# Linear attention and a gated feed-forward block on one core: both halves of the second batch turned by DMA, its work and the loads around it moved to other slots

## Chip, cores and metric

One Trainium2 chip, one core. The metric is the device time of one execution of the whole program, in microseconds (us). Each kernel is executed several times and the median is given. The profile is of one execution.

## What is computed

There are two stages. The first is attention with the keys and values projected along the sequence from 1024 to 64 rows. Its result, 8192 tokens of 512 values, is the input of a gated feed-forward block.

```python
k_proj = np.einsum('ks,bhsd->bhkd', E, k)           # q, k, v: 8 x 8 x 1024 x 64, f32
v_proj = np.einsum('ks,bhsd->bhkd', F, v)
scores = scale * np.matmul(q, k_proj.transpose(0, 1, 3, 2))
scores = scores - np.max(scores, axis=-1, keepdims=True)
attn = np.exp(scores)
attn = attn / (np.sum(attn, axis=-1, keepdims=True) + 1e-09)
attn_out = np.matmul(attn, v_proj)
x = attn_out.transpose(0, 2, 1, 3).reshape(8192, 512)
g = x @ w_gate                                      # 512 x 1536
silu = g * (1.0 / (1.0 + np.exp(-g)))
out = (silu * (x @ w_val)) @ w_out                  # 1536 x 512, f32 out
```

## The kernel before

**The loop that everything hangs on.** The feed-forward part is cut into 16 chunks of 512 tokens, two for each of the 8 batches, and each chunk into 12 column blocks of 128. So there are 192 steps `t`; chunk `c` is `t // 12`. Chunks 0 and 1 are batch 0, chunks 2 and 3 batch 1, and so on. A step does four matmuls of 512 columns for the gate (`f_g`, L324, tile gps), then four for the value (`f_v`, L324, tile vps), and then zero to two portions of four matmuls for the output of the chunk before (`f_y`, L362, tile yps). ScalarE takes a tanh of gps (L336), VectorE makes the hidden tile hT from it (L343, L348). When three portions are done, ScalarE copies the block to ysb (L372), and SyncE (SP) writes it to DRAM (L374).

**Slots.** Attention for the coming batches is spread over the steps by hand. Slot `2t` is run between `f_g` and `f_v` of step `t`, slot `2t+1` after its output portions. `put(s, fn, ...)` lays a unit into slot `s`. The program runs under a manual schedule, so each engine's queue is in the order in which the program is written down; only semaphores order engines against one another. Within a slot, loads come first and the rest in the order of the calls of `put`. Units, each for a batch b and a half ch or an eighth j (four eighths to a half):

- `load_k`, `load_v`, `load_q`: loads with a cast from f32 to bf16, issued by GpSimd (POOL) at L88, L98 and L107. k and v have 1 MB each after the cast, a half of q 0.5 MB. All go through the queue that the profile calls q0, software_dynamic. The weights (L117, L123) go through it as well, ahead of the steps. Buffers: two for k, two for v, four for halves of q.
- `u_KV`: projects k, v or both (L149). ScalarE copies the k part to `ks`, VectorE the v part to BDV.
- `u_KT`: four small transposes of `ks` on TensorE (L174), and four VectorE copies to BD.
- `u_T`: four transposes of 128x128 of q on TensorE into the tile qTp (L195), and a copy to the tile qT by ScalarE.
- `u_TD`: the same turn of a whole half of q by one DMA issued from SP (L207), to the tile qTd.
- `u_S`: four score matmuls with 128 columns (L229) with qT or qTd as weights, and an exponential on ScalarE (L233, tile ee).
- `u_R`: row sums and reciprocals on VectorE (L244, L246). `u_N`: the normalisation on POOL (L260), to the tile AA for one eighth, or AAd for a whole half.
- `u_A`: four transposes of AA on TensorE into the tile aTp (L276), and a copy to AT by VectorE.
- `u_AD`: the same turn of a whole half by one DMA issued from SP (L214), from AAd to AT.
- `u_PV`: one matmul of 512 columns (L287) with BDV as weights, and a copy to xT, the input of the feed-forward part, by ScalarE.

SP's queue thus holds turns and output blocks in program order, and POOL's queue holds normalisations and load issues in program order. An instruction that waits holds up all that stand behind it in its own queue. The DMA turns go through the same queue as the output blocks, the profile's q1, hardware_dynamic.

**Which halves are turned how.** `BY_DMA` lists the halves that go through `u_TD` and `u_AD`. Its trailing `[1:]` leaves out (1, 0): the first half of the second batch goes through `u_T` and `u_A` on TensorE, as all of batch 0 does; the other 13 halves are turned by DMA. `place(b)` puts a batch's units into slots. Chunk 2, the first to need batch 1, begins at slot 48.

Of the kernel before, what the change touches and what calls it, by code (L numbers as in the profile page):

```python
# [15 lines left out]
B = 8  # L16
# [11 lines left out]
CH = 2  # L28
CW = 512
NIT = B * CH * NFT  # L30
BY_DMA = [(b, ch) for b in range(1, B) for ch in range(CH)][1:]


@with_exitstack
def kernel(
# [49 lines left out]
    def load_k(b, h0=0, h1=H):  # L85
        if b:
            kb[b] = kv_pool.tile([P, H, NJ, D], BF16, name="kb", tag="kb")
        nc.gpsimd.dma_start(  # L88
            out=kb[b][:, h0:h1].rearrange("p h j d -> p h (j d)"),
            in_=k[b, h0:h1].rearrange("h (p j) d -> p h (j d)", j=NJ),  # L90
        )
# [11 lines left out]
    def load_q(b, ch, js=(0, 4)):  # L103
        if js[0] == 0:
            qb[b, ch] = q_pool.tile([P, H, 4, D], BF16, name="qb", tag="qb")
        js = slice(*js)
        nc.gpsimd.dma_start(  # L107
            out=qb[b, ch][:, :, js, :].rearrange("p h j d -> p h (j d)"),
            in_=q[b].rearrange("h (p c j) d -> p c h j d", c=2, j=4)[:, ch, :, js, :].rearrange(
                "p h j d -> p h (j d)"  # L110
            ),
        )

    def load_w_gv(c0, c1, which=(0, 1)):
        cs = slice(c0 * P, c1 * P)
        for wsrc, wdst in [((moe_w_gate, wg), (moe_w_val, wv))[i] for i in which]:
            nc.gpsimd.dma_start(  # L117
                out=wdst[:, :, cs],
                in_=wsrc[:, cs].rearrange("(t p) c -> p t c", p=P),
            )  # L120

    def load_wo(i):
        nc.gpsimd.dma_start(  # L123
            out=wo[:, 6 * i : 6 * (i + 1), :],
            in_=moe_w_out[6 * i * P : 6 * (i + 1) * P, :].rearrange("(t p) c -> p t c", p=P),
        )
# [5 lines left out]
    def bank(where, shape, dt, name):  # L132
        pool, tag = banks[where]
        return pool.tile(shape, dt, name=name, tag=tag)
# [85 lines left out]
    def u_S(b, u, at="a"):  # L220
        ch, w = divmod(u, 4)
        g, i = divmod(w, 2)
        ps = bank(at, [P, 4, P], FP32, "sc")
        if (b, ch) in BY_DMA:
            t = qT[b, ch, "d"][:].rearrange("p (h i) t -> p i h t", i=2)[:, i, 4 * g : 4 * g + 4]
# [23 lines left out]
    def u_N(b, u):  # L249
        ch, w = divmod(u, 4)  # L250
        g, i = divmod(w, 2)
        if (b, ch) in BY_DMA:
            if (b, ch, "d") not in AA:
# [62 lines left out]
    def f_mm(c, f, w, i=None):  # L316

        if i != 1:
            half[c, f, w] = bank("gv"[w], [P, CW], FP32, "gv"[w] + "ps")
        ps = half[c, f, w]  # L320
        x = xT[divmod(c, CH)]
        ts = slice(0, CW) if i is None else slice(256 * i, 256 * (i + 1))
        for kt in range(NKT):
            nc.tensor.matmul(  # L324
                out=ps[:, ts],
                lhsT=(wg, wv)[w][:, kt, f * P : (f + 1) * P],
                rhs=x[:, kt, ts],
                start=(kt == 0),
                stop=(kt == NKT - 1),
            )  # L330
        return ps
# [57 lines left out]
    def put(s, fn, *a):  # L389
        slots[s].append((fn, a))  # L390

    def place(b):
        s0 = 48 * (b - 1)
        if b == 1:
            put(30, u_TD, 1, 1)
            put(34, u_KV, 1, "k")
            put(36, u_KT, 1)
            put(40, u_KV, 1, "v")
            sa = (37, 38, 39, 40, 48, 50, 52, 54)
            tt = (35, 36, 37, 38)  # L400
            ta = (41, 42, 43, 44)
            put(57, u_AD, 1, 1)
            sp = (43, 44, 45, 46, 66, 67, 68, 69)
        else:
            put(s0, u_KV, b)
            put(s0 + 3, u_KT, b)
            o = 14 if b == 2 else 6
            put(s0 + (3 if b == 2 else -6), u_TD, b, 0)
            put(s0 + (5 if b == 2 else -4), u_TD, b, 1)
            sa = [s0 + o + 3 * j for j in range(NJ)]  # L410
            put(sa[3] + 4, u_AD, b, 0)
            put(sa[7] + 4, u_AD, b, 1)
            sp = [s0 + i for i in (39, 41, 43, 45, 57, 59, 61, 63)]
        for j in range(NJ):
            if (b, j // 4) not in BY_DMA:
                put(tt[j], u_T, b, j)
                put(ta[j], u_A, b, j)
            put(sa[j], u_S, b, j)
            put(sa[j] + 1, u_R, b, j)
            put(sa[j] + 1, u_N, b, j)  # L420
        for i in range(8):
            put(sp[i], u_PV, b, i // 4, i % 4)
# [5 lines left out]
    with tc.manual_schedule():  # L428
# [99 lines left out]
        load_q(0, 1)  # L528
        for f in (6, 8, 10):
            load_w_gv(f, f + 2)  # L530
        load_wo(0)
        load_wo(1)
        load_k(1)
        f_mm(0, 0, 0, 0)
        u_PV2(0, 0, 1, 1, act)
        f_mm(0, 0, 1, 0)
# [10 lines left out]
        put(22, u_PV, 0, 1, 1)  # L547
        put(23, u_PV, 0, 1, 2)
        put(23, u_PV, 0, 1, 3)
        put(20, load_q, 1, 0)  # L550
        put(20, load_v, 1)
        put(20, load_q, 1, 1)
        for b in range(1, B):
            place(b)
        for b in range(2, B):
            s0 = 48 * (b - 1) - (12 if b == 2 else 24)
            put(s0, load_k, b)
            put(s0 + 2, load_v, b)
            put(s0 + 4, load_q, b, 0)
            put(s0 + 6, load_q, b, 1)  # L560

        for s in slots:
            slots[s].sort(key=lambda x: x[0] not in (load_k, load_v, load_q))
# [50 lines left out]
```

The softmax here doesn't subtract the row's maximum and nothing guards it: scores larger than these inputs give would overflow.

## Time and profile before

| what | value |
|---|---|
| median of 4 runs | 572.75 us (572.51 to 573.37) |
| the profiled execution, its own time | 572.75 us |
| its span, first to last instruction | 571.0 us |
| granted TensorE clock in it | 1.0 |
| DVE, ACT, POOL busy | 336.4, 238.3, 109.1 us |
| read from and written to DRAM | 60.29 and 16.78 MB |
| transposes of L195, of L276 | 48 matmuls each |
| DMA turns of L207, of L214 | 13 each |

How to read it. PE is TensorE's matmul side, PEld its loading of weights, DVE VectorE, ACT ScalarE. A timeline row gives the start, the time until the last of its instructions ended, the engine, line, operation, tiles written and read, and how many instructions are in it. Matmuls are pipelined: a row's own length overlaps the row after it, so what a group costs is the distance between its start and the next row's start. For a DMA, the row of the issuing engine tells when it was issued; landing is when its semaphore says that the data is there.

### The profile page before, as it was taken

What the parts mean: (1) busy time and instruction counts of PE and PEld (TensorE: products, weight loads), DVE (VectorE), ACT (ScalarE), POOL (GpSimd) and SP (SyncE); (2) the same over time, 40 slices, a digit from 0 to 9 for tenths busy, and PEclk for the clock granted to TensorE, in tenths of its full rate; (3) what the DMA queues carried; (4) which work ended last, traced back from release to release, by engine and by line L of the source; (5) the groups of instructions that cost most, each with busy time, mean ns of one, the idle gap of its engine ahead of it and who ended that gap; (6) DMA issues with size and microseconds to landing.
All of it is one profiled execution on the core that took longest, in us unless ns stands there. A gap on an engine that the chain in (4) does not pass through costs nothing.

```text
span 571.0 us, 7944 instructions
## 1 busy us (share of the span) xinstructions
PE 564.1 (99%) x2971; PEld 268.5 (47%) x2971; DVE 336.4 (59%) x581; ACT 238.3 (42%) x421; POOL 109.1 (19%) x122
## 2 busy tenths in 40 slices
PE   8999999999999999999999999999999999999997
PEld 4654444444444444444444444444444444444444
DVE  4777466666466654666556664567546675554540
ACT  3565534344435434443335434354343543443232
POOL 6834122134002500124001330023200220000000
PEclk9999999999999999999999999999999999999999
DMA  9999994349902697038940499204990124100012
GB/s 208 178 200 206 201 170 83 87 80 197 201 18 54 106 190 150 19 74 137 195 94 37 69 175 197 59 20 93 189 184 32 46 48 75 38 37 25 32 38 92
DMA packets 106983, 61.86 MB, mean 108 GB/s; under 512 B 60096, under 2 KB 98240, under 8 KB 106944
## 3 DMA queue, kind: packets, MB, share of 16 engines
q0 software_dynamic: 42800, 29.36, 35.8%
q1 hardware_dynamic: 63232, 30.42, 24.8%
q10 hardware_dynamic: 912, 1.57, 0.9%
q8 instruction: 23, 0.38, 0.3%
q14 instruction: 16, 0.13, 0.1%
HBM read 60.29 MB, written 16.78 MB: 135 GB/s over the span
## 4 chain that ended last, share of the span: by engine, by line
PE 92%; DMA 3%; DVE 2%; POOL 1%; ACT 1%; issue 0%; DVEq 0%; POOLq 0%
PE yps L362 29%; PE vps L324 28%; PE gps L324 27%; PE kvp L149 3%; PE sc L229 2%; PE pv L287 2%; DMA wv<-in_moe_w_val_dram 2%; DMA qb<-in_q_dram 1%; DVE zz L244 1%; POOL AA L260 0%; POOL wg L117 0%; PE qTp L195 0%; DVE hT L348 0%; ACT xT L137 0%; DVE s L343 0%
## 5 line engine op out<-in xcount | busy, mean ns | idle before, releaser
L343 DVE SCALAR_TENSOR_TENSOR s<-th,gps 128x512 f32<-128x512 f32 x192 | 130.5, 680 | 139.0 <-ACT th L336 138.6
L324 PE MATMUL gps<-xT,wg 128*128 128x512 bf16 (+1 forms) x776 | 197.8, 377 | 0.4 <-DMA wg<-in_moe_w_gate_dram 0.2
L324 PE MATMUL vps<-xT,wv 128*128 128x512 bf16 (+1 forms) x776 | 197.5, 377 | 0.1
L362 PE MATMUL yps<-wo,hT 128*128 128x512 bf16 (+1 forms) x780 | 194.5, 376 | 0.0
L336 ACT ACTIVATE th<-gps 128x512 f32<-128x512 f32 x192 | 114.6, 597 | 163.1 <-PE gps L324 161.6
L348 DVE TENSOR_TENSOR hT<-s,vps 128x512 bf16<-128x512 f32 x192 | 131.9, 687 | 22.1 <-PE vps L324 1.5
L362 PEld LDWEIGHTS <-hT 128*128 128x128 bf16 x780 | 76.2, 98 | 89.9
L260 POOL TENSOR_TENSOR AAd<-ee,rr 128x512 bf16<-128x512 f32 x52 | 54.1, 1040 | 319.5 <-issue 178.1
L324 PEld LDWEIGHTS <-wv 128*128 128x128 bf16 x776 | 73.8, 98 | 83.2 <-issue 3.3
L324 PEld LDWEIGHTS <-wg 128*128 128x128 bf16 x776 | 74.0, 98 | 81.6 <-DMA wg<-in_moe_w_gate_dram 0.7
L372 ACT ACTIVATE ysb<-yps 128x512 f32<-128x512 f32 (+1 forms) x65 | 38.4, 591 | 78.1 <-PE yps L362 78.1
L137 ACT CAST xT<-pv 128x512 bf16<-128x512 f32 x63 | 36.7, 585 | 51.2 <-PE pv L287 50.3
L244 DVE TENSOR_REDUCE zz<-ee 128x8 f32<-128x512 f32 x64 | 43.4, 679 | 19.4 <-ACT ee L233 19.4
L233 ACT ACTIVATE ee<-sc 128x512 f32<-128x512 f32 x64 | 37.9, 595 | 17.9 <-PE sc L229 17.8
L287 PE MATMUL pv<-AT,BDV 128*128 128x512 bf16 x60 | 22.6, 379 | 0.0
L229 PEld LDWEIGHTS <-qTd 128*128 128x128 bf16 x208 | 16.0, 98 | 12.3
L229 PE MATMUL sc<-BD,qTd 128*128 128x128 bf16 x208 | 20.1, 219 | 0.0
L137 DVE CAST BDV<-kvp 64x256 bf16<-64x256 f32 x14 | 6.0, 427 | 22.1 <-ACT ks L159 19.1
L260 POOL TENSOR_TENSOR AA<-ee,rr 128x512 bf16<-128x512 f32 x11 | 11.4, 1039 | 36.3 <-ACT th L336 18.7
L246 DVE RECIPROCAL rr<-zz 128x8 f32<-128x8 f32 x64 | 13.0, 203 | 6.7 <-DVE zz L244 0.5
L149 PE MATMUL kvp<-vb,FT 128*64 128x512 bf16 (+2 forms) x80 | 15.7, 339 | 0.3 <-ACT BDV L137 0.3
L149 PE MATMUL kvp<-kb,ET 128*64 128x512 bf16 (+1 forms) x72 | 15.5, 358 | 0.2 <-DMA kb<-in_k_dram 0.2
(51 smaller groups left out, 146.1 us busy)
## 6 DMA issues: line engine op xcount, KB each, us to landing
out_dram<-ysb SPq DMA_DIRECT2D x63, 256.0 KB, 2.3
qb<-in_q_dram POOLq DMA_DIRECT2D x15, 512.0 KB, 17.0
kb<-in_k_dram POOLq DMA_DIRECT2D x7, 1024.0 KB, 11.7
vb<-in_v_dram POOLq DMA_DIRECT2D x7, 1024.0 KB, 14.3
wo<-in_moe_w_out_dram POOLq DMA_DIRECT2D x2, 768.0 KB, 15.5
wg<-in_moe_w_gate_dram POOLq DMA_DIRECT2D x5, 256.0 KB, 9.3
wv<-in_moe_w_val_dram POOLq DMA_DIRECT2D x5, 256.0 KB, 9.9
kraw<-in_k_dram ACTq DMA_DIRECT2D x2, 512.0 KB, 4.8
```

What stands on the lines that cost most here:

```text
L137: (nc.scalar.copy if eng is nc.scalar else eng.tensor_copy)(out=out, in_=in_)
L149: nc.tensor.matmul(out=t[lo : lo + 64, h0:h1].rearrange("p h d -> p (h d)"), lhsT=w[:, j, :], rhs=src[b][:, h0:h1, j, :], start=(j == 0), ...
L229: nc.tensor.matmul(out=ps[:, n, :], lhsT=t[:, n, :], rhs=BD[b % 2][:, 4 * g + n, :], start=True, stop=True)
L233: nc.scalar.activation(out=e[:].rearrange("p h j k -> p (h j k)"), in_=ps[:].rearrange("p a k -> p (a k)"), func=AF.Exp, scale=scale,)
L244: nc.vector.reduce_sum(out=z[:], in_=e[:], axis=AX.X)
L260: eng.tensor_tensor(out=a.rearrange("p j h k -> p h j k"), in0=ee.pop((b, u))[:], in1=rr.pop((b, u))[:].unsqueeze(3).to_broadcast([P, 4, 2 ...
L324: nc.tensor.matmul(out=ps[:, ts], lhsT=(wg, wv)[w][:, kt, f * P : (f + 1) * P], rhs=x[:, kt, ts], start=(kt == 0), stop=(kt == NKT - 1),)
L336: nc.scalar.activation(out=th[:], in_=ps[:], func=AF.Tanh, scale=0.5)
L343: nc.vector.scalar_tensor_tensor(out=s1[:], in0=th[:], scalar=1.0, in1=g[:], op0=ALU.add, op1=ALU.mult)
L348: nc.vector.tensor_tensor(out=hT[c][:, f, :], in0=s1[:], in1=ps[:], op=ALU.mult)
L362: nc.tensor.matmul(out=yy[c][:, cs], lhsT=hT[c][:, f, i * P : (i + 1) * P], rhs=wo[:, f, cs], start=(f == 0), stop=(f == NFT - 1),)
L372: nc.scalar.activation(out=ysb[:, cs], in_=yy[c][:, cs], func=AF.Copy, scale=0.5)
```

## The change

`BY_DMA` loses its `[1:]`, so the first half of batch 1 is turned by DMA too. The units of batch 1 get other slots: its k projection slot 29 in place of 34, the turn of ks 32 in place of 36, the scores of its first half 35 to 38 in place of 37 to 40, those of its second half 41 to 44 in place of 48, 50, 52 and 54, the products with v of its first half 44, 45, 46, 46 in place of 43 to 46. Two new DMA turns are put in slots 22 and 41, and the second turn of normalised values moves from 57 to 47. Batch 2's projections go from slots 48 and 51 to 56 and 59, its turns of q from 51 and 53 to 57 and 59, its scores begin at 61 in place of 62.

The loads move in POOL's queue. The first half of q and the k of batch 1 are issued ahead of the two loads of `wo`; before, k came after them and q at slot 20. The loads of batch 2 go from slots 36 to 42 to slots 43 to 45. In the order of POOL's queue the k and v of batch 2 now stand behind the fifth normalisation of batch 1, the first half of its q behind the sixth, the second half behind the seventh. Before, its k and v stood ahead of all normalisations of batch 1. Batch 3's loads go four slots later.

In SP's queue the order from the start of the steps is now: turn of q (1,0), turn of q (1,1), two output blocks, turn of AAd (1,0), two output blocks, turn of AAd (1,1), an output block, turn of q (2,0), an output block, turn of q (2,1). Before, it was: turn of q (1,1), four output blocks, turn of q (2,0), an output block, turn of q (2,1), turn of AAd (1,1).

```diff
-BY_DMA = [(b, ch) for b in range(1, B) for ch in range(CH)][1:]
+BY_DMA = [(b, ch) for b in range(1, B) for ch in range(CH)]
...
         if b == 1:
+            put(22, u_TD, 1, 0)
+            put(29, u_KV, 1, "k")
+            put(32, u_KT, 1)
+            put(40, u_KV, 1, "v")
+            sa = (35, 36, 37, 38, 41, 42, 43, 44)
+            put(41, u_AD, 1, 0)
             put(30, u_TD, 1, 1)
-            put(34, u_KV, 1, "k")
-            put(36, u_KT, 1)
-            put(40, u_KV, 1, "v")
-            sa = (37, 38, 39, 40, 48, 50, 52, 54)
-            tt = (35, 36, 37, 38)
-            ta = (41, 42, 43, 44)
-            put(57, u_AD, 1, 1)
-            sp = (43, 44, 45, 46, 66, 67, 68, 69)
+            put(47, u_AD, 1, 1)
+            sp = (44, 45, 46, 46, 66, 67, 68, 69)
         else:
-            put(s0, u_KV, b)
-            put(s0 + 3, u_KT, b)
-            o = 14 if b == 2 else 6
-            put(s0 + (3 if b == 2 else -6), u_TD, b, 0)
-            put(s0 + (5 if b == 2 else -4), u_TD, b, 1)
+            put(s0 + (8 if b == 2 else 0), u_KV, b)
+            put(s0 + (11 if b == 2 else 3), u_KT, b)
+            o = 13 if b == 2 else 6
+            put(s0 + (9 if b == 2 else -6), u_TD, b, 0)
+            put(s0 + (11 if b == 2 else -4), u_TD, b, 1)
...
         for j in range(NJ):
-            if (b, j // 4) not in BY_DMA:
-                put(tt[j], u_T, b, j)
-                put(ta[j], u_A, b, j)
...
+        load_q(1, 0)
+        load_k(1)
         load_wo(0)
         load_wo(1)
-        load_k(1)
...
-        put(20, load_q, 1, 0)
         put(20, load_v, 1)
         put(20, load_q, 1, 1)
...
         for b in range(2, B):
-            s0 = 48 * (b - 1) - (12 if b == 2 else 24)
-            put(s0, load_k, b)
-            put(s0 + 2, load_v, b)
-            put(s0 + 4, load_q, b, 0)
-            put(s0 + 6, load_q, b, 1)
+            s0 = 48 * (b - 1) - (20 if b == 3 else 24)
+            at = (43, 43, 44, 45) if b == 2 else (s0, s0 + 2, s0 + 4, s0 + 6)
+            put(at[0], load_k, b)
+            put(at[1], load_v, b)
+            put(at[2], load_q, b, 0)
+            put(at[3], load_q, b, 1)
```

## The prediction

> **What bounds the kernel now.** I read four views in this order: the page, for which engine is full; the groups by shape, for the operations that the change removes; TensorE's timeline between 61 and 80 us, for what one of them costs; SP's and POOL's timelines with the DMA queues by window, for the new turns.
>
> ```profile
> PE 564.1 (99%) x2971; PEld 268.5 (47%) x2971; DVE 336.4 (59%) x581; ACT 238.3 (42%) x421; POOL 109.1 (19%) x122
> ...
> PE 92%; DMA 3%; DVE 2%; POOL 1%; ACT 1%; issue 0%; DVEq 0%; POOLq 0%
> ```
>
> First line: TensorE is busy for 99% of the span of 571.0 us, no other engine for 60%. Second line: the chain that ended last is 92% TensorE. What is not lies in the first 33 us, where weights land. TensorE's waits between 60 and 571 us hold no entry on the matmul side. So every matmul removed after 33 us is gained at the distance that it takes in the queue, and every microsecond that a matmul waits for a late transfer is lost in full.
>
> ```profile
> L195 PE MATMUL qTp<-ident_bf,qb 128*128 128x128 bf16 x48 | 4.7, 220 | 0.2 <-DMA qb<-in_q_dram 0.2
> L276 PE MATMUL aTp<-ident_bf,AA 128*128 128x128 bf16 x48 | 4.7, 220 | 0.3 <-POOL AA L260 0.2
> ...
> 61.77 0.39 PE L195 MATMUL qTp<-ident_bf,qb 128*128 128x128 bf16 x4
> 61.99 1.03 PE L324 MATMUL gps<-xT,wg 128*128 128x512 bf16 x4
> ...
> 74.47 0.39 PE L276 MATMUL aTp<-ident_bf,AA 128*128 128x128 bf16 x4
> 74.69 1.03 PE L324 MATMUL gps<-xT,wg 128*128 128x512 bf16 x4
> ```
>
> A group of four transposes starts at 61.77 and the next matmul at 61.99: it costs 0.22 us, not 4 x 220 ns, because matmuls overlap.
>
> ```profile
> 62.38 7.22 SPq L207 DMA_TRANSPOSE qTd<-qb  x1
> ...
> 86.99 2.34 SPq L207 DMA_TRANSPOSE qTd<-qb  x1
> ...
> 125.03 7.94 SPq L214 DMA_TRANSPOSE AT<-AAd  x1
> ...
> q0 software_dynamic: 814, 0.82, 123.3%
> ...
> q0 software_dynamic: 947, 0.96, 93.9%
> q1 hardware_dynamic: 856, 0.22, 27.6%
> ```
>
> The three turns landed 13.0, 4.4 and 17.6 us after their issue (each asked for alone); the first and third ran beside loads. The last rows count packets, MB and time: loads alone from 42 to 46 us, then loads beside a turn from 66 to 72. Loads alone move 814/4 = 203 packets a us; beside a turn 947/6 = 158, and the turn 856/6 = 143 of 256 B (0.22 MB/856). A turn of 0.5 MB has about 2,050 such packets, so some 14 us beside loads, and takes 22% of the loads' pace meanwhile: 14.3 x 0.22 = 3.2 us.
>
> **The change, part by part.**
>
> *Removed from TensorE.* Four groups L195 at 61.77, 63.17, 65.36 and 66.67 take 0.22 + 0.24 + 0.22 + 0.22 = 0.90 us to the next row; four groups L276 at 74.47, 75.55, 78.37 and 79.67 take 0.22 + 0.23 + 0.22 + 0.22 = 0.89. Sum: -1.79 us. All other matmuls stay in number and shape; they only change places. The Trainium skill, "TensorE: Matmul & The Clock Gate", Part 4, puts a transpose of this size at about 275 ns in a kernel. By that the 32 would be worth 8.8 us and the span about 562; the rows above say 0.22 us for four, and I go by them.
>
> *Removed elsewhere.* Four ScalarE copies of about 0.58 us and four VectorE copies of about 0.4 us: nothing, as both engines have room (42% and 59%) beside TensorE.
>
> *Added: two DMA turns, and moved loads.* They cost nothing if each transfer lands before its reader's turn on TensorE. I set one against the other. Reader times are those of before, less the transposes gone by then and plus the units moved ahead.
>
> 1. First half of q, batch 1. The last weight block ahead of it was issued at 26.79 and landed 12.7 later, at 39.5; 0.5 MB takes 2.6 us (v landed at 59.7, the next half of q at 62.4), so it lands at 42.1. SP has nothing ahead, so its turn goes out there, beside loads: 13.0 to 17.6 us, at 55.1 to 59.7. Reader: the first score, slot 35, where the first L195 row stands, 61.8 plus 0.3 for the turn of ks: 62.1. Margin 2.4 to 7.
> 2. k of batch 1: 42.1 + 5.1 = 47.2, about 48 with the turn beside it from 45 on. Reader: slot 29, after the values of step 14 (51.19 + 0.86): 52.0. Margin 4.
> 3. `wo`: two of 0.77 MB. Before, these and k and q ended at 54.6; with at most 3.2 more, 57.8. The second is read from 60.4 on, the first (about 53) at 57.7. Margin 2.6.
> 4. v of batch 1: 59.7 + 3.2 = 62.9; read at 70.0. The second half of q: 62.4 + 3.2 = 65.6. Its turn is issued by SP then; behind it in SP's queue stand two output blocks and the turn of AAd, and the first block is ready about 62.6, so it waits 3 us, which a third ysb buffer covers. No load is in the queue any more, since batch 2's k stands behind the fifth normalisation (76.9 at the earliest). So the idle price, 4.4 to 5.0: lands at 70.0 to 70.6. Reader: the fifth score in slot 41, 74.47 - 0.88: 73.6. Margin 3.
> 5. Turn of AAd (1,0): the fourth score comes at 66.2. From score to the end of its normalisation the first half took 3.3 to 6.2 us before (65.13 to 68.43, 69.48 to 75.69), so 69.5 to 72.4; idle price 4.2 to 5.6: 73.7 to 78.0. Reader: the first product with v, slot 44: 79.67 less 0.88, 0.66 and 0.22, plus four scores of 0.22: 78.8. Margin 0.8 to 5.
> 6. Loads of batch 2: k issued 76.9 to 79.8, moving 1.6 later (k at 120.88 showed its first packets about 122), 5.1 each: v at 88.6 to 91.5. Read in slot 56: step 24 starts at 85.72 - 1.79 + 0.88 = 84.8, four steps of 2.59 and a gate later 96.1. Margin 4.6.
> 7. Turn of q (2,0) stands in SP's queue behind the turn of AAd (1,1) (issued about 86, after an output block) and one block. AAd (1,1) runs beside q's loads: 13.0 to 17.6, taken 13 to 15, done at 99 to 101; behind it the idle 4.4: 103.4 to 105.4. Reader: slot 61, 84.8 + 6 x 2.59 + 2.3 (projection and turn of ks) + 2.6: 105.2. Margin 1.8 to -0.2. By the full 17.6 it would be 108.0, a loss of 2.8.
>
> The same skill's "DMA: Bandwidth & Descriptors", Latency and other measured facts, gives a DMA transpose 261 GB/s: an estimate of 2.0 us for 0.5 MB, by which item 7 would be some 9 us early (q at 94 at the latest, plus 2.0, against 105.2). The rows say 4.4 idle and 13.0 or more loaded; with either the sum is the same.
>
> Batches 3 to 7 keep their units' places, with batch 3's loads about 5 us later: its k landed at 132.3 (issue 120.9 + 11.5), its projection stands at 155.6. Covered.
>
> *Sum.* 572.75 - 1.79 + 0 = 570.96, say 571.0. The profiled execution took 572.75, span 571.0 and 1.75 outside it, equal to the median; the span should become 569.2. Each wait is nothing at its nearest row, at the far ends 0.2 to 2.8 us (item 7) and up to 10 (item 5 at 17.6).
>
> **The rivals.**
>
> *A part of the gain is given back at batch 2's turn of q (item 7), or a similar stall of 0.7 to 2.9 us.* For it: three DMA turns in a row share the queue with 3 MB of loads, and one landed after 17.6. Against: only q's last MB is left when AAd (1,1) starts. At 2 us of stall: 571.0 + 2.0 = 573.0; at the far end 573.8.
>
> *Slower: the turn of AAd (1,0) is late for the product with v (item 5).* In place of eight short TensorE operations there is a chain score, exponential, sums, normalisation, SP, DMA. For it: the smallest lower margin, and the rows beside loads; if batch 2's k slips in beside it, it lands 13.0 to 17.6 after 69.5 to 72.4, at 82.5 to 90, and TensorE stands 3.7 to 11.2 us. From a landing at 78.8 it costs; from 80.6 the gain is gone. Against: k can't be issued before the fifth score, some 7 us after the fourth. At a landing of 84: 571.0 + 5.2 = 576.2.
>
> *Hidden anyway: the transposes filled gaps where TensorE would have waited, so the time stays at 572.7.* Against: the rows follow one another without a gap around all eight groups. For: nothing that I saw.
>
> **How the numbers follow.** No stall over 0.6 us: 0.66; time 571.0, with 0.3 to each side from the spread of the runs and the reading of the distances. Part given back: 0.13. Hidden: 0.04. Slower by a late turn: 0.17. A measurement of this kernel can tell 0.2%, 1.15 us, from no change: the first case is faster, the second and third are within, the fourth is slower: 0.66, 0.17, 0.17. The range reaches from 570.4 through the part given back to 573.5; what is left out is the slower case.
>
> **What would show it.** 32 matmuls at L195 and L276 each, 14 turns at L207 and L214 each. No wait of TensorE at L229 for qTd or at L287 for AT after 60 us. The first turn landing between 55 and 60, its successor near 70. The step 24 gate at 84.8 in place of 85.7. Wrong would be: a matmul-side wait in batch 1 or 2, or rows that stand as far apart as before without the transposes.

## The result, and the profile after

| | before | after |
|---|---|---|
| median (lowest to highest, runs) | 572.87 us (572.46 to 574.09, 49) | 571.79 us (571.27 to 573.46, 31) |
| ratio of times, 95% interval | | 0.9981 (0.9976 to 0.9986) |
| profiled execution, its span | 572.75, 571.0 us | 571.73, 570.0 us |
| granted TensorE clock | 1.0 | 1.0 |

The kernel became 1.08 us faster, 0.19%. The interval leaves out 1, but the gain falls just short of the 1.15 us that the prediction had set as its bound for a change that can be told. Foretold were 571.0 us and a span of 569.2; the range of 570.4 to 573.5 holds the result.

First the page of the changed kernel (engine busy times and the chain that ended last), then its groups by shape.

```profile
PE 562.7 (99%) x2939; PEld 266.4 (47%) x2939; DVE 334.8 (59%) x577; ACT 236.6 (42%) x417; POOL 109.2 (19%) x122
...
PE 92%; DMA 3%; DVE 2%; POOL 1%; ACT 1%; issue 0%; ACTq 0%; DVEq 0%; POOLq 0%
```

```profile
L276 PE MATMUL aTp<-ident_bf,AA 128*128 128x128 bf16 x32 | 3.1, 220 | 0.3 <-ACT AT L137 0.2
L195 PE MATMUL qTp<-ident_bf,qb 128*128 128x128 bf16 x32 | 3.1, 220 | 0.0
```

The 32 matmuls are gone, 16 at each line, and TensorE is still busy for 99% of the span. Its waits between 34 and 560 us hold no entry on the matmul side in this profile, so no new transfer made it wait.

**Where the gain is.** I set one matmul row of the chain that ended last, the projection of batch 3, against the same row of the kernel before, and did the same late in the program. The columns are start, length, and what ran. First before, then after:

```profile
155.59 1.85 PE kvp L149 x16
...
427.41 1.85 PE kvp L149 x16
```

```profile
154.22 1.85 PE kvp L149 x16
...
426.03 1.85 PE kvp L149 x16
```

Both rows stand 1.37 to 1.38 us earlier. That is the 1.79 us foretold, less 0.41 us that had been lost before the change's first step was reached. TensorE's timeline at the wait for a weight block (in brackets the idle time and what ended it) and at the last values ahead of the first moved unit, before and then after:

```profile
32.04 1.04 PE L324 MATMUL gps<-xT,wg 128*128 128x512 bf16 x4 [0.17 <-DMA wg<-in_moe_w_gate_dram]
...
51.19 1.03 PE L324 MATMUL vps<-xT,wv 128*128 128x512 bf16 x4
```

```profile
32.48 1.04 PE L324 MATMUL gps<-xT,wg 128*128 128x512 bf16 x4 [0.32 <-DMA wg<-in_moe_w_gate_dram]
...
51.59 1.03 PE L324 MATMUL vps<-xT,wv 128*128 128x512 bf16 x4
```

The weights land about 0.4 us later, and the lateness stays (0.41 us before rounding at the second row). So, in this pair of profiles, the changed kernel enters the changed stretch 0.41 us late and leaves it 1.38 us early: 1.79 us gained within it, the sum's term to the hundredth.

**What is lost behind the last output.** The last output block, which ScalarE issues, goes out 1.38 us earlier (568.31 before, 566.93 after; ScalarE's timeline) and lands 1.38 us earlier (569.99, 568.61), but the span ends only 1.02 us earlier (570.97, 569.95). SP's waits from 560 us on, before and then after; the columns are the sum, the number and the longest, in us:

```profile
SPq L609 <- DMA out_dram<-ysb: 3.2, 3, 1.3
```

```profile
SPq L607 <- DMA out_dram<-ysb: 3.6, 1, 3.6
```

At its end SP asks eight DMA semaphores one after the other, 0.06 us each (after: 568.63, 568.69 and so on to 569.06). Before, the last block was on the seventh, so one more was asked after it (the expectation printed below says two). After, with two DMAs more in the program, it is on the first: SP waits once, for 3.6 us, and then asks seven more. Six more by 0.06 us are 0.36 us: -1.79 + 0.41 + 0.36 = -1.02, which is the profiled difference.

**The transfers.** SP's timeline of the changed kernel; SP's row gives the issue, and where the row has x2, it holds two of the same kind:

```profile
42.13 25.68 SPq L207 DMA_TRANSPOSE qTd<-qb  x2
67.87 2.73 SPq L374 DMA_DIRECT2D out_dram<-ysb  x2
71.38 1.91 SPq L214 DMA_TRANSPOSE AT<-AAd  x1
78.70 7.68 SPq L374 DMA_DIRECT2D out_dram<-ysb  x2
86.49 6.28 SPq L214 DMA_TRANSPOSE AT<-AAd  x1
93.83 0.33 SPq L374 DMA_DIRECT2D out_dram<-ysb  x1
99.06 4.08 SPq L207 DMA_TRANSPOSE qTd<-qb  x1
```

And the rows of TensorE that read what these turns bring:

```profile
62.51 0.39 PE L229 MATMUL sc<-BD,qTd 128*128 128x128 bf16 x4
...
73.98 0.39 PE L229 MATMUL sc<-BD,qTd 128*128 128x128 bf16 x4
...
79.19 0.38 PE L287 MATMUL pv<-AT,BDV 128*128 128x512 bf16 x1
...
105.64 0.39 PE L229 MATMUL sc<-BD,qTd 128*128 128x128 bf16 x4
```

| transfer | issued | landed | reader | margin, us |
|---|---|---|---|---|
| turn of q (1,0) | 42.13 | 61.32 (19.2) | 62.51 | 1.2 |
| turn of q (1,1) | 66.11 | 70.38 (4.3) | 73.98 | 3.6 |
| turn of AAd (1,0) | 71.38 | 75.62 (4.2) | 79.19 | 3.6 |
| turn of AAd (1,1) | 86.49 | 101.24 (14.7) | 112.14 | 10.9 |
| turn of q (2,0) | 99.06 | 105.15 (6.1) | 105.64 | 0.5 |
| load of v, batch 2 | 78.14 | 94.66 | 96.55 | 1.9 |

No margin is negative. The smallest, 0.5 us, is at the place that the prediction had given the smallest.

### The profile page after: what moved, and what is told of

It reads as the page before. It is cut to its first block, busy times and chain, and to the rows that moved or that the text cites. A ratio compares the mean times of both kernels' runs of the same rounds, so it can differ in the third digit from the quotient of the medians.

```text
span 570.0 us, 7879 instructions
## 1 busy us (share of the span) xinstructions
PE 562.7 (99%) x2939; PEld 266.4 (47%) x2939; DVE 334.8 (59%) x577; ACT 236.6 (42%) x417; POOL 109.2 (19%) x122
## 4 chain that ended last, share of the span: by engine, by line
PE 92%; DMA 3%; DVE 2%; POOL 1%; ACT 1%; issue 0%; ACTq 0%; DVEq 0%; POOLq 0%
PE yps L362 29%; PE vps L324 28%; PE gps L324 27%; PE kvp L149 3%; PE sc L229 2%; PE pv L287 2%; DMA wv<-in_moe_w_val_dram 2%; DMA kraw<-in_k_dram 1%; DVE zz L244 1%; POOL AA L260 0%; POOL wg L117 0%; DVE hT L348 0%; ACT xT L137 0%; DVE s L343 0%; PE kTp L174 0%
## 5 line engine op out<-in xcount | busy, mean ns | idle before, releaser
L260 POOL TENSOR_TENSOR AAd<-ee,rr 128x512 bf16<-128x512 f32 x56 | 58.2, 1041 | 343.3 <-issue 157.2
L229 PEld LDWEIGHTS <-qTd 128*128 128x128 bf16 x224 | 17.2, 98 | 13.2
L229 PE MATMUL sc<-BD,qTd 128*128 128x128 bf16 x224 | 21.7, 219 | 0.0
L107 POOL DMA_DIRECT2D qb<-in_q_dram x17 | 15.6, 919 | 0.6 <-DMA wv<-in_moe_w_val_dram 0.6
```

The source lines that it names most:

```text
L229: nc.tensor.matmul(out=ps[:, n, :], lhsT=t[:, n, :], rhs=BD[b % 2][:, 4 * g + n, :], start=True, stop=True)
L260: eng.tensor_tensor(out=a.rearrange("p j h k -> p h j k"), in0=ee.pop((b, u))[:], in1=rr.pop((b, u))[:].unsqueeze(3).to_broadcast([P, 4, 2 ...
```

## The experiments

**Theories.** T: the transposes are worth 1.79 us on TensorE, the covers hold, and two small terms at the two ends of the program, which no late turn makes, take back about 0.8. The rivals: the transposes are worth less than their distance in the queue; or the moved loads cost something; or the new places of the loads do nothing and the transfers were never near to deciding.

**What 32 transposes cost.** In the changed kernel, eight groups of four transposes are put back, of data that is there already; nothing reads their result.

```diff
+        def dummy(n):
+            ps = bank("a", [P, 4, P], BF16, "dmy")
+            for i in range(4):
+                nc.tensor.transpose(
+                    out=ps[:, i, :],
+                    in_=qb[1, 0][:, n, 0:2, :].rearrange("p j d -> p (j d)"),
+                    identity=ident_bf[:],
+                )
+
+        for n, s in enumerate((35, 36, 37, 38, 41, 42, 43, 44)):
+            put(s, dummy, n)
```

> The changed kernel with eight groups of four transposes put back on TensorE in slots 35 to 38 and 41 to 44, whose results nobody reads: the output is unchanged. Theory (a group costs 0.22 us on the path, and nothing else of the change moves the steps): 8 x 0.22 = 1.79 more, 571.79 + 1.79 = 573.6, which is over the kernel before by the part that was lost at start and end. Rival (the transposes sat in gaps, and the gain came from the moved units): 571.8 to 572.2. By 0.275 us for each transpose: 8.8 more, 580.6.

Measured: 573.37 us (572.94 to 573.75), 1.58 more than the changed kernel; ratio to before 1.0009 (1.0 to 1.0018). TensorE's timeline:

```profile
62.63 0.39 PE L229 MATMUL sc<-BD,qTd 128*128 128x128 bf16 x4
62.85 0.39 PE L563 MATMUL dmy<-ident_bf,qb 128*128 128x128 bf16 x4
63.08 1.03 PE L324 MATMUL gps<-xT,wg 128*128 128x512 bf16 x4
```

The dead group starts at 62.85 and the next row at 63.08: 0.23 us. Two rows that the changed kernel has at 51.59 and 154.22, the first from the same timeline and the second from the chain that ended last, stand here at:

```profile
51.72 1.03 PE L324 MATMUL vps<-xT,wv 128*128 128x512 bf16 x4
...
156.13 1.85 PE kvp L149 x16
```

TensorE is 0.13 us late ahead of the eight groups and 1.91 behind them: 1.78 us. So the first term of the sum is shown, by putting its cost back alone. What the Trainium skill ("TensorE: Matmul & The Clock Gate", Part 4) gives for one such transpose, 275 ns, makes by estimate 580.6 us of this kernel; here the measurement decides.

**The moved loads alone.** The kernel before, with the loads of q and k of batch 1 ahead of those of `wo`:

```diff
+        load_q(1, 0)
+        load_k(1)
         load_wo(0)
         load_wo(1)
-        load_k(1)
...
-        put(20, load_q, 1, 0)
```

> The kernel before with the changed order of loads alone: the first half of q and the k of batch 1 ahead of wo, and no other change. Theory (moved loads cost nothing, as each still lands ahead of its reader): 572.9, within 0.2 us. Rival (the reordered issue shifts the start or delays the weights): up to 0.5 us more; the step 0 values then start at 33.8 in place of 33.4.

Measured: 572.98 us (572.81 to 573.74), ratio 1.0001 (0.9992 to 1.001). The order of these loads costs nothing by itself that can be told, and the gate's row behind the weight wait stands at 32.31 here.

**The last semaphore.** Seven tiny loads from SP late in the changed kernel, so that the last output block comes on the eighth semaphore; two in the kernel before, so that it comes on the first, as in the changed one. They write to a tile that is no longer read.

```diff
+        def tiny(n):
+            nc.sync.dma_start(out=ef[0][0:1, 8 * n : 8 * n + 8], in_=E[0:1, 8 * n : 8 * n + 8])
+
+        for n in range(7):
+            put(340 + 2 * n, tiny, n)
```

> The changed kernel with seven tiny loads (32 bytes each, data that is there already) put into SP's queue in slots 340 to 352, so that the last output block's DMA takes the eighth of the eight hardware DMA semaphores, which SP asks for last at the end, in place of the first. Theory (0.36 us of the missing 0.7 is lost at the end: SP asks the eight in a fixed order, 0.06 us each, and with two more DMAs the last block fell on the first of them, so seven are asked after its landing; before, two were): from the last landing to the end of the span 1.0 us in place of 1.4, time 0.43 us less than the changed kernel's 571.79, 571.4. Rival (what is missing was lost to waits in batches 1 and 2, or is scatter): 571.8. The start also tells something: if the 0.4 us that the changed kernel's profile is late at the first full matmuls of the steps (33.82 against 33.42) belongs to the program, it is there again; if it is scatter, it need not be.

> The kernel before with two tiny loads in SP's queue in slots 340 and 342, so that its last output block falls on the first of the eight semaphores, as in the changed kernel. Theory of the end: 0.37 us more than before, 572.87 + 0.37 = 573.2, 1.4 us from the last landing to the end. Rival: 572.9. The start is before's: value matmuls of step 0 at 33.4 if the start belongs to the program.

Measured: changed kernel with seven 571.56 us (571.10 to 571.79), ratio to before 0.9976 (0.9966 to 0.9985); kernel before with two 573.17 us (572.93 to 573.86), ratio 1.0006 (0.9997 to 1.0014). SP's waits from 560 us on, first of the changed kernel with seven, then of the kernel before with two:

```profile
SPq L613 <- DMA out_dram<-ysb: 3.2, 3, 1.3
```

```profile
SPq L615 <- DMA out_dram<-ysb: 3.6, 1, 3.6
```

The two kernels have changed rows: the changed one now has the three waits, the one before the single wait of 3.6 us. In the kernel before with two, 1.35 us lie between the last landing (569.95) and the end (571.30), where there were 0.98. Within the span the step is shown both ways: by the medians over the runs it went from 570.0 to 569.6 in the one and from 571.1 to 571.4 in the other. In the time it isn't settled: 571.56 against the 571.79 of another set is 0.2 us, and the interval of the kernel with two takes in no change. Outside the span the seven loads raised the time from 1.78 to 1.99 us, so that only half of what the span gained came out; in the kernel before with two it stayed at 1.77.

**Again, in a third set.** To see how much of this repeats, the two unchanged kernels and the one with seven tiny loads were run once more; the changed one had one single run besides.

> The changed kernel once more, for a second profile of its start. If the late start (value matmuls of step 0 at 33.8 in place of 33.4) belongs to the program: 33.8 again. If it is scatter of the first landings: anywhere from 33.3 to 33.9, and from that point on the same distances as in the first profile.

> The kernel before once more, unchanged. If the late start belongs to the changed program, this one's value matmuls behind the last early weights start at 33.3 to 33.6 us, as in two profiles of it or of its tail variant (33.42, 33.39), and the changed kernels' of this call at 33.8 or later. If it is scatter, the two overlap. Time 572.9.

> The changed kernel a third time. From 34 us to the last output's copy the distances are those of its first profile. Start by program: 33.8 to 34.0, time 1.1 under the kernel before. Start by scatter: anywhere from 33.4 to 34.1, time 1.1 to 1.4 under it (1.79 for the transposes less 0.37 for the end).

> The changed kernel with the seven tiny loads once more, beside the unchanged one on the same chip: 0.43 us under it if the end alone makes the difference, 0.2 as in the first comparison across calls, or nothing if the end of the span doesn't count in the time.

Measured: the kernel before 572.89 us (572.57 to 573.35), ratio to itself 0.9999 (0.999 to 1.0008); the changed kernel 571.62 (571.34 to 572.70), ratio 0.9976 (0.9967 to 0.9986); with seven tiny loads 571.56 (571.10 to 572.81), ratio 0.9976 (0.9965 to 0.9986); the single run 571.91. Of the 0.3 us that the span gained by the seven loads in this set (569.85 to 569.55) the time outside it took back nearly all (1.76 to 2.06). So there is no version here that beats the changed kernel by an amount that can be told.

This set also tells how far the loss at the start repeats. Its profiles of the two kernels have the values at 51.58 and 51.71, and the projection of batch 3 at 156.05 and 154.33: 0.13 us late ahead of the change, 1.72 early behind it. The gain within the stretch is there again, and the loss ahead of it is a third of what it was. By the medians the changed kernel is 1.37 us under the kernel before (572.99 in this set) and 1.27 under its repeat, where it had been 1.08 in the first set.

The start, in all profiles: the first row of the gate behind the weight wait stands at 32.02 to 32.41 us in the kernel before, its repeat and its two variants, and at 32.46 to 32.79 in the changed kernel, its repeats and the variants of it with tiny loads, dead transposes or earlier scores. Two variants of the changed kernel don't fit: 32.23 with q's load at slot 20, and 32.01 with batch 2's loads early, though that one has the changed order of the first loads. The first load of all, E, which is issued ahead of anything that the change touches, lands at 5.73 to 5.90 us in the former and mostly at 6.01 to 6.15 in the latter, but at 5.79 with the dead transposes, whose gate row is late all the same. The repeat of the kernel before, at 32.41 (its values at 33.80, where 33.3 to 33.6 was expected if the program sets the start), is nearer to the changed kernel than to the first profile of its own. So what sets this third of a microsecond stays open, and also whether it belongs to the change.

**The place of batch 2's loads.** The changed kernel with batch 2's loads back in slots 36 to 42, ahead of batch 1's normalisations:

```diff
-            s0 = 48 * (b - 1) - (20 if b == 3 else 24)
-            at = (43, 43, 44, 45) if b == 2 else (s0, s0 + 2, s0 + 4, s0 + 6)
+            s0 = 48 * (b - 1) - ({2: 12, 3: 20}.get(b, 24))
+            at = (s0, s0 + 2, s0 + 4, s0 + 6)
```

> The changed kernel with the loads of batch 2 at their old slots 36, 38, 40 and 42, so that its k stands ahead of batch 1's normalisations in POOL's queue and its v and q between them. Theory (a DMA turn beside loads takes 13 to 19 us in place of 4.3, and TensorE then waits for it): the second turn of q, issued at 66.1, lands at 79 to 85 in place of 70.4; its reader is due at 74.0, so a wait of 5 to 11 us at L229; the turn of AAd behind it in the same queue is late too, a further wait at L287. Time 577 to 590. Rival (the place of these loads doesn't matter, the gain is the transposes alone): 571.8.

Measured: 585.56 us (584.53 to 586.47), ratio 1.0219 (1.0204 to 1.0235). TensorE's waits:

```profile
PE pv L287 <- DMA AT<-AAd: 6.6, 1, 6.6
PE sc L229 <- DMA qTd<-qb: 4.1, 1, 4.1
```

The turn of q (1,1) took 11.7 us in place of 4.3, that of AAd (1,0) 19.4 in place of 4.2, and TensorE waited 10.7 us. The time rose by 13.8. The windows show where the rest is; the columns are the stretch, its length, the busy time of PE, PEld, DVE, ACT and POOL, then PEclk, DMA share and GB/s:

```profile
73.00:78.00 5.00, 0.87 (x6) 0.26 (x5) 1.19 (x2) 0.00 (x0) 0.00 (x0) 0.95 1.44 126
78.00:82.00 4.00, 4.00 (x19) 2.03 (x18) 1.88 (x4) 1.68 (x3) 1.04 (x1) 0.64 1.20 239
86.00:91.00 5.00, 0.00 (x0) 0.00 (x0) 0.08 (x1) 0.00 (x0) 0.72 (x1) 0.67 1.46 164
91.00:95.00 4.00, 3.53 (x9) 1.38 (x11) 1.30 (x3) 0.59 (x1) 0.00 (x0) 0.56 0.37 73
```

In the second and fourth rows TensorE has work again, but at a clock of 0.64 and 0.56: the granted clock was 0.5 from 77.47 to 80.89 us and from 87.71 to 94.54. TensorE was at work for 3.05 us of the one (from 77.84) and 3.3 of the other (from 91.25), and half of that, 3.2 us, is lost; 10.7 + 3.2 = 13.9. This variant is the slower rival of the prediction, made real by letting batch 2's k in beside the turns.

**The first turn, later.** The old order of the loads, q at slot 20:

```diff
-        load_q(1, 0)
-        load_k(1)
         load_wo(0)
         load_wo(1)
+        load_k(1)
...
+        put(20, load_q, 1, 0)
```

> The changed kernel with the old order of loads: wo, wo, k of batch 1, and the first half of q at slot 20 again. Theory: the first half of q lands at 54.6 in place of 42.1, its turn goes out then, beside v and the second half of q (1.5 MB, some 10 us with the turn), and lands 11 to 14 us later at 66 to 68; the first score is due at 62.5, so TensorE waits 3 to 6 us at L229: 575 to 578. Rival (the order of loads costs and gains nothing): 571.8. Its start has the old order of loads: value matmuls of step 0 at 33.4 if the order makes the start, and anywhere from 33.3 to 33.9 if that is scatter of the first landings.

Measured: 575.76 us (574.87 to 577.09), ratio 1.0057 (1.004 to 1.0073). TensorE's timeline in the profiled execution, which took 574.87:

```profile
65.61 0.40 PE L229 MATMUL sc<-BD,qTd 128*128 128x128 bf16 x4 [3.15 <-DMA qTd<-qb]
```

q landed at 54.52, its turn took 11.0 us, to 65.57, and the first score waited 3.15 us; 571.73 + 3.15 = 574.88. The clock in this profile was not lowered by the wait (1.00 from 62 to 66 us). The two longest of the four runs have mean clocks of 0.996 and 0.997, the two shortest 0.999 and 1.0, so there the longer waits may have lowered it; they have no profile. The change of load order, which costs nothing alone, is what makes the first turn fit.

**The first score, one slot sooner.**

```diff
-            sa = (35, 36, 37, 38, 41, 42, 43, 44)
+            sa = (34, 35, 36, 37, 41, 42, 43, 44)
```

> The changed kernel with the first four scores of batch 1 one slot sooner (34 to 37). Theory (the first turn of q landed at 61.32, 1.2 us ahead of its reader at 62.51; one slot sooner the reader is due about 59.9): a wait of about 1.4 us at L229 for qTd, time 571.8 + 1.4 = 573.2. Rival (the landing has some us to spare, as the prediction's 55 to 60 said): 571.8.

Measured: 572.56 us (571.44 to 574.29), ratio 0.9993 (0.9983 to 1.0004). TensorE's waits have one entry at this place:

```profile
PE sc L229 <- DMA qTd<-qb: 0.7, 1, 0.7
```

The turn landed at 61.05, 17.9 us after its issue, and the score waited 0.7 us where I had expected 1.4; the time is 0.8 over the changed kernel's, not 1.4. A slot sooner takes all of the first turn's margin, so slot 35 is the first that holds. The wide spread of the runs fits a landing that varies by a microsecond or two from run to run; that was not profiled.

## Why the prediction was right, and where it wasn't

**Right.**

- The transposes are worth 1.79 us: the rows from 34 us to the last output copy move by just that, and the dead transposes give 1.78 back.
- The covers hold in what was profiled. TensorE has no wait on the matmul side from 35 to 560 us in the changed kernel, its two repeats, and the versions with tiny loads or dead transposes; the rivals "part given back" and "late turn" didn't happen, "hidden anyway" is excluded by the dead transposes. Whether the covers hold in every run is not shown. Of 59 runs of the changed kernel, with and without the tiny loads, four have a mean granted clock of 0.996 or 0.997 and took 572.70 to 573.46 us, a microsecond or more over the median. Of the 100 runs of the kernel before and its two variants that have a clock on record, none is below 0.999. A late transfer that lets the clock fall, as with q at slot 20, would fit; none of the four has a profile.
- The loads moved ahead of `wo` cost nothing by themselves that can be told (572.98 against 572.93).
- Items 2 and 3: k landed at 47.64 and the two `wo` at 52.65 and 57.73 (about 48, 53 and 57.8 foretold). Items 4, 5 and 7: the second turn of q landed at 70.38 (70.0 to 70.6 foretold), that of AAd (1,0) at 75.62 (73.7 to 78.0), that of q (2,0) at 105.15 (103.4 to 105.4) with a margin of 0.5 (1.8 to -0.2). The idle price was 4.2 to 4.3 us (4.4 to 5.0). The gate of step 24 stands at 85.23 (84.8), late by the 0.41 us of the start. The mechanism of the slower rival is real as well: 13.8 us when batch 2's loads get in beside the turns.

**Sizes that were off, with the time left as it was.**

- Item 1: "13.0 to 17.6 us, at 55.1 to 59.7". It took 19.2 us and landed at 61.32, so the margin was 1.2 and not 2.4 to 7. The 14 us worked out for the packets themselves were right, as the DMA queues of the changed kernel between 46 and 58 us show (packets, MB, share of the engines' time):

```profile
q0 software_dynamic: 1874, 1.88, 91.9%
q1 hardware_dynamic: 1835, 0.47, 29.4%
```

  In 12 us that is 156 load packets a microsecond and 153 turn packets, one for one. But the turn's first packets came at about 46 us, 3.9 after its issue, and loads stood beside it to its end. Its last packets came between 59.7 and 60.3, and it landed a microsecond behind them. Neither row that I took as a bound had loads of this kind beside it to its end. Beside the turn of 13.0 us they had run out: 27 load packets from 73 to 75, and 964 in the turn's queue. Beside that of 17.6 us they became smaller: from 137 to 141 there went 864 load packets of 0.54 KB each on average and 864 in the turn's queue, 216 a microsecond of each.
- Item 6: batch 2's v landed at 94.66, not 88.6 to 91.5. By windows of the DMA queues, loads began slowly (151 packets in the four microseconds to 81), ran at 1327 in 8 us, 166 a microsecond, from 83 to 91 with output blocks between them, and shared with the turn of AAd (1,1) from 91 on (340 load packets and 338 turn packets to 93). The item had taken 1.6 us to the first packets and 203 a microsecond from there. Margin 1.9, not 4.6.

**Where luck comes in.** By its first case alone, 571.0 with 0.3 to each side, the prediction would have missed 571.79. The range holds the time because it was drawn up to 573.5 for a stall at item 7, and that stall did not come.

**The step that was off** is the sum, "572.75 - 1.79 + 0 = 570.96". The zero was argued for everything between 33 us and the last output. It was also put, without a word, on what lies ahead of and behind that. Behind the last output, 0.36 us were given back because two DMAs more move the last block to another semaphore; that is shown in the span, by moving it both ways. Ahead of 33 us, 0.41 us were lost in the profiled execution, and 0.13 in the pair of the third set; the cause is open. In the first pair the two together took 0.77 of 1.79 us.

## What to carry to other kernels

A DMA turn has no price of its own: the same 0.5 MB took 4.2 us alone and up to 19.4 beside loads, so moving work from a full TensorE to the DMA pays only together with the places of the loads around it. A group of small transposes in a full TensorE queue is worth its issue distance (0.22 us for four), not the sum of its lengths. When the expected gain is a few tenths of a per cent, the first and the last microseconds need terms of their own in the sum.

## What the runs showed of the hardware

- **Waiting TensorE can lose its clock.** In the kernel with batch 2's loads early, the granted clock fell to 0.5 about 3.8 us into the first wait (73.7 to 77.47) and 3.0 us into the second (84.7 to 87.71), and came back 3.05 and 3.3 us after work had begun again. A wait of 3.15 us in another kernel left it at 1.00. The Trainium skill, "TensorE: Matmul & The Clock Gate", What's actually happening, states a halved clock after an idle window of about 3.4 us, and the full clock after such a window of work, with the windows running free of the kernel. The trace agrees with it in the length: the four changes of the clock (77.47, 80.89, 87.71 and 94.54) lie 3.4, 6.8 and 6.8 us apart, one and twice two windows. But by that length the window that ended at 87.71 had begun at 84.30, and TensorE worked until 84.7: a window with 0.4 us of work in it counted as idle here. So a wait near 3 us may or may not lose the clock.
- **Late transfers therefore cost more than their wait:** 10.7 us of waits cost 13.8.
- **The order of semaphores at the end** is worth up to 0.4 us of the span by which of eight the last output falls on, at 0.06 us each.
- **The span is not all of the time.** The seven tiny loads shortened the span by 0.3 to 0.4 us and lengthened what lies outside it by 0.2 to 0.3, in both sets; why is open.
